# A gated-MLP times attention kernel: the order of the tiles and of their block sums ahead of the large product, and the lead of the last stage's loads

## The chip, the cores and the metric

The kernel runs on one core of one Trainium2 chip. The metric is the device time of one launch in microseconds, the median of the runs shown. A core has five engines with a queue of instructions each: TensorE (PE in the profile, with its weight loads as PEld), VectorE (DVE), ScalarE (ACT), GpSimd (POOL) and SyncE (SP), which here only issues the transfers. An engine takes its instructions in the order of its queue; an instruction at the head of a queue that has to wait holds up all those behind it.

## The reference

With x of 2048 rows by 512 columns, all in fp32:

```python
xn = _layernorm(x, axis=-1)
s = _A_ref(xn, A_k_cache, A_v_cache, A_wq, A_wo)      # attention: 32 heads, the last 512 keys
g = _silu(_B_ref(xn, B_w_in, B_w_sp, B_b_sp, B_w_out))
return x + s * g

def _B_ref(x, w_in, w_sp, b_sp, w_out):               # Fh = 688
    z = _gelu(jnp.einsum("bsd,df->bsf", x, w_in))
    z1 = z[..., :Fh]
    z2 = _layernorm(z[..., Fh:], axis=-1)
    g = jnp.einsum("ts,bsf->btf", w_sp, z2) + b_sp[None, :, None]
    return jnp.einsum("bsf,fd->bsd", z1 * g, w_out)
```

The change touches only B, from the computation of z2 on: z2 is 2048 x 688, w_sp is 2048 x 2048, w_out is 688 x 512.

## The kernel before, in words

A product of two fp32 operands is done with three matmuls: each operand is written as a high part (a cast to the matmul's type) and a low part (the operand less its high part), and high x high, high x low and low x high are summed. The cast is always done on ScalarE; the low part is always a subtraction in the helper of line 59, on VectorE or on GpSimd. So L59 stands for low parts of all kinds, and is told apart by shape and engine.

The order of the work is written out by hand: the order in which the code calls the operations is the order in each engine's queue. A table `ev` holds work by a time t (`on(t, f, ...)`); `step(t)` runs what stands under t. t counts the slots of the sweep (below), and the tiles of the z stage have the negative t, from -16 to -1.

**The z stage**, to 1509.9 us. 16 tiles of 128 rows, in the order of the list `ZO`: the lower half (tiles 8 to 15) first, then the upper half (0 to 7). A tile has two halves of 344 columns, each with 12 matmuls into a PSUM bank. ScalarE takes a half out of its bank with the gelu (L787), VectorE takes its statistics (L788, joined in L794). After every second tile, GpSimd computes 1/sqrt(var + eps) for the pair (L74, L75). The pairs of the lower half are then normalised on VectorE, in place (L802). For the pairs of the upper half GpSimd computes a shift (L804), and ScalarE normalises with it one tile later (`z_apply`, L809). Another tile later `z_split` makes high and low parts of the pair's left columns (L815 on ScalarE, L59 on GpSimd, tile `b`, 128x688).

**The sweep**, L873, 1509.9 to 1730.7 us. w_sp and z2 are cut into 2 x 2 blocks, called A11 to A22 and B11 to B22, and the product of the two is made of seven products of blocks (P1 to P7) in place of eight. For these, sums and differences of blocks are needed: T1, T2, T3, T4 on the side of z2 (`t_diff`, L887, on VectorE; `t_split`, L892 on ScalarE and L59), and sums of A blocks on the other (`a_sum`). Each block of z2 is held in four pieces j = 0 to 3 of two tiles of rows. The lower half of z2's rows gives B21 and B22, the upper half B11 and B12, so a difference of the two halves needs a piece of each. `t_diff` and `t_split` of the pieces stand in the event table.

The sweep has 56 slots (`SLOTS`), each of one product P and one tile of rows: 24 matmuls, eight pieces of three, into one of six banks `ps`. The first four slots multiply by B21 (P2), the next four by B11 (P1). A slot's operand of w_sp is prepared two slots ahead (`prep`: L858, cast on ScalarE, and L59 with 128x1024 elements on VectorE; for slots 0 and 1 the low part is done on GpSimd, in the z stage). `evict` takes the result of a slot out, at the following slot (L991 on ScalarE for P1, else VectorE). Finished rows of the gated product, u, are stored to `u_dram` (L979).

**The projection**, 1730.9 to the end. 16 tiles of rows in the order `PO`: tile n needs its rows of u, of s and of x. `load_p` fetches them with six transfers that SP issues (four of L1052 for u, one each of L1053 and L1054 for s and x) into a buffer of the pool `x8`, which has eight. `split_u` transposes u on VectorE (L1062, L1063) and makes high and low parts; `project` is 17 matmuls into a bank `ps_f`; `finish_out` is a Silu on ScalarE (L1082), a product on VectorE (L1083) and a sum on GpSimd (L1084), which leave the result in the tile's x8 buffer; `send_out` stores it from there (L1087). The first loads are issued in the last slots of the sweep, the others one for each tile.

The loop over the tiles at the end reads:

```python
for n, i in enumerate(PO):
    if n + 6 < NT: load_p(PO[n + 6])
    if n + 2 < NT: split_u(PO[n + 2])
    ...
    project(i); finish_out(i, nc.gpsimd)
    if n: send_out(PO[n - 1])
```

Of the kernel before, what the change touches and what calls it, by code (L numbers as in the profile page):

```python
# [12 lines left out]
OP = mybir.AluOpType  # L13
# [7 lines left out]
NT = S // P  # L21
# [13 lines left out]
T8 = NT // 2  # L35
# [5 lines left out]
def mixer_kernel(ctx: ExitStack, tc: tile.TileContext, x, wh, w_in, w_sp, b_sp, w_out, out):  # L41
# [8 lines left out]
    nc = tc.nc  # L50
# [101 lines left out]
    mv, rx, tmp = {}, {}, {}  # L152
# [391 lines left out]
    T0, T1 = -QL, NSTEP + OL  # L544
# [68 lines left out]
    n, t = 0, 28  # L613
# [138 lines left out]
    att.close()  # L752


    ZO = list(range(T8, NT)) + list(range(T8))
    RP = NT // 2
    HW = RP * P
    ctx.enter_context(tc.tile_pool(name="gap", bufs=1, side="right")).tile([P, 88], F32, name="gap")
    br = ctx.enter_context(tc.tile_pool(name="br", bufs=20, side="right", reuse_waits="tile"))
# [30 lines left out]
    def z_norm(pos):  # L790
        g, j = divmod(pos, 2)
        if j == 0:
            zmv[g] = stats.tile([P, 2, 2], F32, name="mvz")
        nc.vector.bn_aggr(zmv[g][:, j, :], zst[ZO[pos]])  # L794
        if j == 1:
            r = stats.tile([P, 2], F32, name="rz_r")
            tmp = stats.tile([P, 2], F32, name="rz_t")
            rsqrt(zmv[g][:, :, 1], r, 2, tmp)
            for k in range(2):
                t, mean, rs = zt(ZO[pos - 1 + k]), zmv[g][:, k, 0:1], r[:, k:k + 1]  # L800
                if pos < RP:
                    nc.vector.tensor_scalar(t, t, mean, rs, op0=OP.subtract, op1=OP.mult)  # L802
                else:
                    nc.gpsimd.tensor_scalar(tmp[:, k:k + 1], mean, rs, -1.0, op0=OP.mult, op1=OP.mult)  # L804
                    zn.setdefault(pos, []).append((t, tmp[:, k:k + 1], rs))

    def z_apply(pos):
        for t, shift, rs in zn.pop(pos, ()):
            nc.scalar.activation(t, t, AF.Identity, bias=shift, scale=rs)  # L809
# [87 lines left out]
    def on(t, f, *args):  # L897
        ev.setdefault(t, []).append((f, args))
# [3 lines left out]
    def step(t):  # L902
        if 1 < t + 2 < NS:
            prep(t + 2, V)
        for f, args in ev.get(t, ()):
            f(*args)

    for j in range(4):
        on((-8, -4, 4, 6)[j], load_halves, "P2", j)
        on((0, 2, 8, 10)[j], load_halves, "P1", j)  # L910
        on(-4 + 2 * j, t_diff, j, "T1")
        on(-4 + 2 * j, t_diff, j, "T3")
        on(-3 + 2 * j, t_diff, j, "T2")
        on(-3 + 2 * j, t_diff, j, "T4")
        on((-2, -1, 2, 4)[j], t_split, j, "T2", G if j == 2 else V)
    for j in range(4):
        on((0, 3, 5, 6)[j], t_split, j, "T1", V)
        on((1, 4, 12, 12)[j], t_split, j, "T3", V)
        on((13, 14, 17, 18)[j], t_split, j, "B22", V)
        on((18, 19, 20, 20)[j], t_split, j, "T4", V)  # L920
    AT = {0: (6, 7, 9, 10, 10, 11), 1: (12, 13, 15, 16, 16, 21), 2: (18, 20, 21, 23, 23, 25)}
    for r in range(RP):
# [6 lines left out]

    for pos, i in enumerate(ZO):  # L930
        for n in (2, 3):
            z_product(i, n)
            z_gelu(i, n)
        z_norm(pos)
        z_apply(pos - 1)
        if pos > 2 and pos % 2:
            z_split(pos - 2)
        if pos == 3:
            for k in ((0, 1), (1, 1)):
                fetch_x(0, k)  # L940
        t = pos - NT
        if t in (-6, -4):
            prep(t // 2 + 3, nc.gpsimd)
        step(t)
    left.close()
    psum.close()
# [143 lines left out]
    for k in range(NF):  # L1090
        on(WHEN[4, "P6"] + 2 if k < 2 else f7, load_wo, k)
        on(f7 + 2 + k // 3, split_wo, k)
    for n, t in enumerate((f7, f7, f7 + 1, f7 + 2, f7 + 3, f7 + 4)):
        on(t, load_p, PO[n])
    on(f7 + 3, split_u, PO[0])
    on(f7 + 4, split_u, PO[1])

    for t in range(NS):
        if t == 0:
            z_apply(NT - 1)  # L1100
        if t == 1:
            z_split(NT - 1)
        if t:
            evict(*SLOTS[t - 1])
        step(t)
        products(t)
# [2 lines left out]
        for f, args in ev.get(t, ()):  # L1109
            f(*args)  # L1110
    for n, i in enumerate(PO):
        if n + 6 < NT:
            load_p(PO[n + 6])
        if n + 2 < NT:
            split_u(PO[n + 2])
        if n == NT - 1:
# [50 lines left out]
```

## Time and profile before

| what | value |
|---|---|
| runs | 1807.52, 1811.16, 1806.87 us; median 1807.52 |
| profiled execution | 1810.7 us |
| its span, first to last instruction | 1808.9 us |
| mean granted clock of TensorE | 0.996 |
| busy: PE, DVE, ACT, POOL | 1775.6, 1491.2, 1177.4, 1260.5 us |
| attention and z1 | 0 to about 1451 us |
| z stage | about 1451 to 1509.9 us |
| sweep (L873) | 1509.9 to 1730.7 us |
| projection, `ps_f` | from 1730.9 us |

Everything up to 1451 us is the same in both kernels, and of no concern here. "The joint" is used below for the first slots of the sweep, where work on the last tiles of z still goes on. A row of the timeline reads: start in us, duration in us, engine, line, operation, tile written <- tiles read, shape, how many in a row; in brackets the idle time ahead of it and what ended it. A row of the table by windows gives for a stretch of time each engine's busy time, the clock granted to TensorE as a share of full speed, the busy share of the DMA engines, and GB/s. Rows of SPq are the issues of transfers on SP.

### The profile page before, as it was taken

Reading aid. Unit: us, or ns where it says so; the run is one execution under the profiler, and the core shown is the slowest. Engines: PE = TensorE matmul, PEld = TensorE weight load, DVE = VectorE, ACT = ScalarE, POOL = GpSimd, SP = SyncE. Lnnn points to the kernel's source line nnn. Section 1 sums busy time; section 2 is a strip of 40 time slices with the busy share of each in tenths; the row PEclk is TensorE's granted clock in tenths of the full one; section 3 lists DMA queues with packets and bytes.
Section 4 is the critical chain, followed back from the end, with each engine's and each line's share of the span. In section 5 each row is a group of like instructions: output and inputs, shape, how many; then the busy total and the mean of one; then the engine's idle time right before and its main releaser. Section 6 shows DMA issues by size and latency. Waiting matters only on the chain.

```text
span 1808.9 us, 28552 instructions
## 1 busy us (share of the span) xinstructions
PE 1775.6 (98%) x8460; PEld 1518.5 (84%) x8460; DVE 1491.2 (82%) x2447; ACT 1177.4 (65%) x2626; POOL 1260.5 (70%) x1199
## 2 busy tenths in 40 slices
PE   8999999999999999899999999999999999999997
PEld 7888888888888887788888888888888998999985
DVE  5689988989998988788888888888888557787774
ACT  4777777767777776577777777777777435443242
POOL 2798898898888987678888888888888324000042
PEclk9999999999999999999999999999999999999999
DMA  5687897988988889787877777777778643645476
GB/s 187 193 237 234 244 273 223 262 251 232 268 250 237 265 236 286 239 264 222 225 226 224 225 216 231 225 221 225 226 224 255 222 140 109 211 152 194 139 217 185
DMA packets 181164, 402.12 MB, mean 222 GB/s; under 512 B 24080, under 2 KB 61200, under 8 KB 161808
## 3 DMA queue, kind: packets, MB, share of 16 engines
q1 hardware_dynamic: 176400, 394.66, 73.5%
q10 hardware_dynamic: 4608, 5.64, 0.9%
q8 instruction: 66, 1.08, 0.2%
q14 instruction: 90, 0.74, 0.1%
HBM read 233.74 MB, written 166.46 MB: 221 GB/s over the span
## 4 chain that ended last, share of the span: by engine, by line
PE 82%; DMA 7%; DVE 4%; ACT 2%; SPq 2%; issue 2%; POOL 1%; ACTq 0%; DVEq 0%; POOLq 0%
PE ps_a L450 14%; PE ps L67 12%; PE ps L65 12%; PE ps L66 11%; PE ps L873 9%; PE ps_a L517 6%; PE ps_a L515 6%; PE ps_a L516 6%; PE ps_a L65 2%; PE ps_a L66 2%; PE ps_a L67 2%; DMA x<-x_dram 1%; DMA p_dram<-pL 1%; DMA pL<-p_dram 1%; DMA out<-x 1%
## 5 line engine op out<-in xcount | busy, mean ns | idle before, releaser
L59 POOL TENSOR_TENSOR pT_l<-pL,pT_h 128x512 fp32r<-128x512 f32 x507 | 658.4, 1302 | 187.5 <-ACT pT_h L507 165.7
L479 ACT ACTIVATE prob<-ps,nm 128x512 f32<-128x512 f32 x512 | 354.0, 691 | 339.7 <-DVE nm L477 332.2
L539 DVE SCALAR_TENSOR_TENSOR sacc<-ps,sums,sacc 128x512 f32<-128x512 f32 x496 | 369.8, 746 | 130.0 <-PE ps L67 124.4
L450 PE MATMUL ps_a<-x,x 128*128 128x512 f32 x1302 | 376.7, 390 | 6.1 <-DMA x<-x_dram 6.1
L488 DVE STREAM_TRANSPOSE pL<-prob 128x512 f32<-128x512 f32 x512 | 358.8, 701 | 3.3 <-ACT prob L479 3.3
L477 DVE TENSOR_REDUCE nm<-ps 128x1 f32<-128x512 f32 x512 | 340.1, 664 | 6.6 <-PE ps L67 6.5
L507 ACT CAST pT_h<-pL 128x512 fp32r<-128x512 f32 x512 | 318.5, 622 | 20.0 <-DMA pL<-p_dram 12.1
L450 PEld LDWEIGHTS ps_a<-x,x 128*128 128x128 f32 x1302 | 244.6, 188 | 58.1 <-DMA x<-x_dram 5.4
L59 POOL TENSOR_TENSOR wl<-raw,wh 128x512 fp32r<-128x512 f32 x186 | 242.0, 1301 | 11.9 <-ACT wh L144 11.9
L873 PE MATMUL ps<-b,x 128*128 128x344 f32 x1344 | 214.9, 321 | 6.2 <-ACT b L991 3.1
L873 PEld LDWEIGHTS ps<-b,x 128*128 128x128 f32 x1344 | 213.3, 189 | 7.7 <-ACT b L991 3.4
L517 PE MATMUL ps_a<-pT_l,wh 128*128 128x512 f32 x512 | 200.2, 391 | 2.3 <-POOL pT_l L59 2.2
L65 PE MATMUL ps<-wh,qT_h 128*128 128x512 f32 x512 | 199.9, 390 | 0.6 <-DVE sacc L539 0.6
L67 PE MATMUL ps<-wh,qT_l 128*128 128x512 f32 x512 | 200.0, 391 | 0.3
L515 PE MATMUL ps_a<-pT_h,wh 128*128 128x512 f32 x512 | 199.9, 390 | 0.0
L65 PE MATMUL ps<-wh,oT_h 128*128 128x512 f32 x512 | 199.7, 390 | 0.0
L66 PE MATMUL ps<-wl,qT_h 128*128 128x512 f32 x512 | 199.5, 390 | 0.0
L67 PE MATMUL ps<-wh,oT_l 128*128 128x512 f32 x512 | 199.5, 390 | 0.0
L66 PE MATMUL ps<-wl,oT_h 128*128 128x512 f32 x512 | 199.4, 390 | 0.0
L516 PE MATMUL ps_a<-pT_h,wl 128*128 128x512 f32 x512 | 199.3, 389 | 0.0
L59 POOL TENSOR_TENSOR b<-b 128x688 fp32r<-128x688 f32 (+1 forms) x11 | 19.2, 1747 | 198.1 <-ACT b L1039 189.7
L59 POOL TENSOR_TENSOR x<-wq,x 128x256 fp32r<-128x256 f32 x186 | 138.8, 747 | 1.5 <-ACT x L432 1.5
(207 smaller groups left out, 3010.8 us busy)
## 6 DMA issues: line engine op xcount, KB each, us to landing
p_dram<-pL SPq DMA_DIRECT2D x128, 1024.0 KB, 4.8
pL<-p_dram SPq DMA_DIRECT2D x256, 192.0 KB, 4.1
raw<-wh SPq DMA_DIRECT2D x188, 256.0 KB, 6.2
pL<-p_dram SPq DMA_DIRECT2D x256, 128.0 KB, 4.0
x<-w_sp SPq DMA_DIRECT2D x24, 1024.0 KB, 5.1
pL<-p_dram SPq DMA_DIRECT2D x256, 64.0 KB, 3.9
wq<-wh SPq DMA_DIRECT2D x62, 256.0 KB, 5.7
x_dram<-rawx SPq DMA_DIRECT2D x32, 256.0 KB, 6.1
```

The lines of the kernel that those rows point to most:

```text
L59: engine.tensor_tensor(lo, whole, hi.bitcast(F32), op=OP.subtract)
L65: nc.tensor.matmul(ps, lh, rh, start=first, stop=False)
L66: nc.tensor.matmul(ps, lh, rl, start=False, stop=False)
L67: nc.tensor.matmul(ps, ll, rh, start=False, stop=last)
L450: nc.tensor.matmul(qps[g, bank], wt["q", g, k][a][:, c * P:(c + 1) * P], X[g * 2 // H][ORDER[k]][:, b, c], start=first, stop=r == 5, skip_ ...
L477: nc.vector.tensor_reduce(nm, ps, axis=AX.X, op=OP.max, negate=True)
L479: nc.scalar.activation(prob[t], ps, AF.Exp, bias=nm, accum_out=sums[b][:, j:j + 1])
L488: nc.vector.transpose(pL[b][:, :, j * P:j * P + P].rearrange("p a (c q) -> p a c q", q=Q), prob.pop(t).rearrange("p (a c q) -> p a c q", a ...
L507: nc.scalar.copy(h, p)
L517: nc.tensor.matmul(pps[b], vh, pl, start=False, stop=c == 3)
L539: nc.vector.scalar_tensor_tensor(at, ps, rs, at, op0=OP.mult, op1=OP.add)
L873: nc.tensor.matmul(ps, a, b, start=k != "P4" and c == 0 and m == 0, stop=c == RP - 1 and m == 2, skip_group_check=True)
```

## The change

In the z stage:

- `ZO` takes pairs of tiles from the two halves in turn: 8, 9, 0, 1, 10, 11, 2, 3 and so on, to 14, 15, 6, 7. After each four tiles, a piece of each half is there.
- Every pair is normalised on ScalarE, with the shift from GpSimd; the normalisation on VectorE (L802 before) is gone.
- The differences of blocks stand at other times: for T1 and T3 at -10, -6, -2 and 3 in place of -4, -2, 0 and 2, for T2 and T4 at -9, -5, -1 and 4 in place of -3, -1, 1 and 3. The splits of T1, T2, T3 and B22 move too, and the one T2 split whose low part was on GpSimd has it on VectorE.
- The low parts of the operands of slots 0 and 1 are made on VectorE in place of GpSimd.
- Two blocks of the normalised x, which the tiles of the upper half multiply, are fetched back from DRAM (`fetch_x`) at position 5 in place of 3.

At the joint, the normalisation and the split of the last pair move from ahead of `evict` and `step` in slots 0 and 1 to events of slots 1 and 2. `step(t)` calls `prep(t + 2)` first, so these stand behind the operands of slots 2 and 3 on ScalarE and, for the split, of slot 4.

In the projection, loads are issued five tiles ahead, not six.

```diff
--- before.py
+++ after.py
@@ -752,8 +752,8 @@
     att.close()
 
 
-    ZO = list(range(T8, NT)) + list(range(T8))
     RP = NT // 2
+    ZO = [i + k for j in range(0, RP, 2) for i in (RP + j, j) for k in range(2)]
     HW = RP * P
     ctx.enter_context(tc.tile_pool(name="gap", bufs=1, side="right")).tile([P, 88], F32, name="gap")
     br = ctx.enter_context(tc.tile_pool(name="br", bufs=20, side="right", reuse_waits="tile"))
@@ -798,11 +798,8 @@
             rsqrt(zmv[g][:, :, 1], r, 2, tmp)
             for k in range(2):
                 t, mean, rs = zt(ZO[pos - 1 + k]), zmv[g][:, k, 0:1], r[:, k:k + 1]
-                if pos < RP:
-                    nc.vector.tensor_scalar(t, t, mean, rs, op0=OP.subtract, op1=OP.mult)
-                else:
-                    nc.gpsimd.tensor_scalar(tmp[:, k:k + 1], mean, rs, -1.0, op0=OP.mult, op1=OP.mult)
-                    zn.setdefault(pos, []).append((t, tmp[:, k:k + 1], rs))
+                nc.gpsimd.tensor_scalar(tmp[:, k:k + 1], mean, rs, -1.0, op0=OP.mult, op1=OP.mult)
+                zn.setdefault(pos, []).append((t, tmp[:, k:k + 1], rs))
 
     def z_apply(pos):
         for t, shift, rs in zn.pop(pos, ()):
@@ -905,18 +902,20 @@
         for f, args in ev.get(t, ()):
             f(*args)
 
+    on(1, z_apply, NT - 1)
+    on(2, z_split, NT - 1)
     for j in range(4):
         on((-8, -4, 4, 6)[j], load_halves, "P2", j)
         on((0, 2, 8, 10)[j], load_halves, "P1", j)
-        on(-4 + 2 * j, t_diff, j, "T1")
-        on(-4 + 2 * j, t_diff, j, "T3")
-        on(-3 + 2 * j, t_diff, j, "T2")
-        on(-3 + 2 * j, t_diff, j, "T4")
-        on((-2, -1, 2, 4)[j], t_split, j, "T2", G if j == 2 else V)
+        on((-10, -6, -2, 3)[j], t_diff, j, "T1")
+        on((-10, -6, -2, 3)[j], t_diff, j, "T3")
+        on((-9, -5, -1, 4)[j], t_diff, j, "T2")
+        on((-9, -5, -1, 4)[j], t_diff, j, "T4")
+        on((-8, -4, 3, 4)[j], t_split, j, "T2", V)
     for j in range(4):
-        on((0, 3, 5, 6)[j], t_split, j, "T1", V)
-        on((1, 4, 12, 12)[j], t_split, j, "T3", V)
-        on((13, 14, 17, 18)[j], t_split, j, "B22", V)
+        on((0, 1, 2, 5)[j], t_split, j, "T1", V)
+        on((0, 1, 2, 12)[j], t_split, j, "T3", V)
+        on((12, 13, 17, 18)[j], t_split, j, "B22", V)
         on((18, 19, 20, 20)[j], t_split, j, "T4", V)
     AT = {0: (6, 7, 9, 10, 10, 11), 1: (12, 13, 15, 16, 16, 21), 2: (18, 20, 21, 23, 23, 25)}
     for r in range(RP):
@@ -935,12 +934,12 @@
         z_apply(pos - 1)
         if pos > 2 and pos % 2:
             z_split(pos - 2)
-        if pos == 3:
+        if pos == 5:
             for k in ((0, 1), (1, 1)):
                 fetch_x(0, k)
         t = pos - NT
         if t in (-6, -4):
-            prep(t // 2 + 3, nc.gpsimd)
+            prep(t // 2 + 3, nc.vector)
         step(t)
     left.close()
     psum.close()
@@ -1090,16 +1089,12 @@
     for k in range(NF):
         on(WHEN[4, "P6"] + 2 if k < 2 else f7, load_wo, k)
         on(f7 + 2 + k // 3, split_wo, k)
-    for n, t in enumerate((f7, f7, f7 + 1, f7 + 2, f7 + 3, f7 + 4)):
+    for n, t in enumerate((f7, f7, f7 + 1, f7 + 2, f7 + 3)):
         on(t, load_p, PO[n])
     on(f7 + 3, split_u, PO[0])
     on(f7 + 4, split_u, PO[1])
 
     for t in range(NS):
-        if t == 0:
-            z_apply(NT - 1)
-        if t == 1:
-            z_split(NT - 1)
         if t:
             evict(*SLOTS[t - 1])
         step(t)
@@ -1109,8 +1104,8 @@
         for f, args in ev.get(t, ()):
             f(*args)
     for n, i in enumerate(PO):
-        if n + 6 < NT:
-            load_p(PO[n + 6])
+        if n + 5 < NT:
+            load_p(PO[n + 5])
         if n + 2 < NT:
             split_u(PO[n + 2])
         if n == NT - 1:
```

Since lines were taken out, line numbers behind them are lower by 3 in the z stage and the sweep (L809 is L806, L858 is L855, L892 is L889), and by 1 in the projection (L1052 is L1051, L1087 is L1086).

**GpSimd around the end of the z stage.** The rows L74, L75 and L804 (L801) are the rsqrt and the shift of a pair; L59 with 128x2x344 is the low part of a piece of z2, L59 with 128x1024 that of an operand of w_sp. Before:

```order
L75 TENSOR_TENSOR rz_r<-rz_t,power 128x2
L804 TENSOR_SCALAR rz_t<-mvz,rz_r 128x1 x2
L59 TENSOR_TENSOR b<-b 128x2x344
L59 TENSOR_TENSOR x_18683<-x_18524,x_18683 128x1024
L74 TENSOR_SCALAR rz_t<-mvz 128x2
L75 TENSOR_TENSOR rz_r<-rz_t,power 128x2
L804 TENSOR_SCALAR rz_t<-mvz,rz_r 128x1 x2
L59 TENSOR_TENSOR b<-b 128x2x344
L74 TENSOR_SCALAR rz_t<-mvz 128x2
L75 TENSOR_TENSOR rz_r<-rz_t,power 128x2
L804 TENSOR_SCALAR rz_t<-mvz,rz_r 128x1 x2
L59 TENSOR_TENSOR b<-b 128x2x344 x3
```

Now:

```order
L59 TENSOR_TENSOR b<-b 128x2x344
L74 TENSOR_SCALAR rz_t<-mvz 128x2
L75 TENSOR_TENSOR rz_r<-rz_t,power 128x2
L801 TENSOR_SCALAR rz_t<-mvz,rz_r 128x1 x2
L59 TENSOR_TENSOR b<-b 128x2x344
L74 TENSOR_SCALAR rz_t<-mvz 128x2
L75 TENSOR_TENSOR rz_r<-rz_t,power 128x2
L801 TENSOR_SCALAR rz_t<-mvz,rz_r 128x1 x2
L59 TENSOR_TENSOR b<-b 128x2x344 x2
```

The operand's low part is gone from this queue. Of the three low parts at the end before, the first two are the third and the fourth piece of B11, and the last is a piece of T2; of the two now, the first is the fourth piece of B21, the block that slot 0 multiplies, and the second the fourth piece of B11. The fourth piece of B21 thus stands behind the rsqrt and shift of the last pair; before, it was done in the middle of the z stage.

**ScalarE at the joint.** L787 is the gelu of a half tile, L809 (L806) the normalisation of a pair, L815 (L812) the high part of a piece of B21 or B11, L892 (L889) that of a difference, L858 (L855) that of a slot's operand. Before, with the operand of slot 2 in the last row:

```order
L787 ACTIVATE b<-ps_18734 128x344
L787 ACTIVATE b<-ps_18751 128x344
L809 ACTIVATE b<-b,rz_t,rz_r 128x2x344 x2
L892 CAST b<-b 128x2x344
L787 ACTIVATE b<-ps_18775 128x344
L787 ACTIVATE b<-ps_18791 128x344
L815 CAST b<-b 128x2x344
L892 CAST b<-b 128x2x344
L809 ACTIVATE b<-b,rz_t,rz_r 128x2x344 x2
L858 CAST x_18836<-x_18689 128x1024
```

Now:

```order
L787 ACTIVATE b<-ps_18752 128x344
L787 ACTIVATE b<-ps_18769 128x344
L806 ACTIVATE b<-b,rz_t,rz_r 128x2x344 x2
L787 ACTIVATE b<-ps_18791 128x344
L787 ACTIVATE b<-ps_18807 128x344
L812 CAST b<-b 128x2x344
L855 CAST x_18847<-x_18706 128x1024
L889 CAST b<-b 128x2x344 x2
L855 CAST x_18883<-x_18706 128x1024
L806 ACTIVATE b<-b,rz_t,rz_r 128x2x344 x2
```

The casts for the operands of slots 2 and 3 now stand ahead of the last pair's normalisation (the last row); before, they stood behind it.

**SP in the projection.** The number behind `x_` tells the x8 buffers' tiles apart; `out<-x_20573` and `out<-x_20581` are the store of tile 0, before and now. Before:

```order
L1052 DMA x_20828<-u_dram 32x4x192 x2
L1052 DMA x_20828<-u_dram 32x4x160 x2
L1053 DMA x_20828<-s_dram 128x512
L1054 DMA x_20828<-x 128x512
L1087 DMA out<-x_20573 128x512
L1052 DMA x_20865<-u_dram 32x4x192 x2
L1052 DMA x_20865<-u_dram 32x4x160 x2
L1053 DMA x_20865<-s_dram 128x512
L1054 DMA x_20865<-x 128x512
L1087 DMA out<-x_20580 128x512
```

Now:

```order
L1086 DMA out<-x_20581 128x512
L1051 DMA x_20866<-u_dram 32x4x192 x2
L1051 DMA x_20866<-u_dram 32x4x160 x2
L1052 DMA x_20866<-s_dram 128x512
L1053 DMA x_20866<-x 128x512
L1086 DMA out<-x_20588 128x512
L1051 DMA x_20903<-u_dram 32x4x192 x2
L1051 DMA x_20903<-u_dram 32x4x160 x2
L1052 DMA x_20903<-s_dram 128x512
L1053 DMA x_20903<-x 128x512
L1086 DMA out<-x_20625 128x512
```

With eight buffers, the load of tile 8 (`x_20865` before, `x_20903` now) takes the buffer of tile 0. Before, the store of tile 0 is the row just ahead of it; now a load and the store of tile 1 stand between the two.

## The prediction

> **What bounds the kernel now.** The page's first part says TensorE, and the windows by stage say where it does not.
>
> ```profile
> span 1808.9 us, 28552 instructions
> ...
> PE 1775.6 (98%) x8460; PEld 1518.5 (84%) x8460; DVE 1491.2 (82%) x2447; ACT 1177.4 (65%) x2626; POOL 1260.5 (70%) x1199
> ```
>
> ```profile
> core 0: us, PE busy (x) PEld busy (x) DVE busy (x) ACT busy (x) POOL busy (x), PEclk, DMA share, GB/s
> 1453.60:1509.94 56.34, 56.34 (x369) 56.34 (x368) 30.73 (x58) 26.53 (x47) 23.75 (x28) 1.00 0.27 94
> 1509.94:1540.00 30.06, 23.81 (x147) 22.39 (x145) 25.28 (x28) 15.32 (x21) 8.12 (x7) 1.00 0.48 149
> 1540.00:1543.40 3.40, 3.40 (x12) 3.40 (x13) 3.35 (x5) 3.40 (x5) 0.00 (x0) 0.50 0.46 184
> 1545.00:1705.00 160.00, 160.00 (x1016) 160.00 (x1015) 126.23 (x148) 60.24 (x67) 0.00 (x0) 1.00 0.52 174
> 1730.90:1769.49 38.59, 38.59 (x171) 31.86 (x171) 27.19 (x51) 15.38 (x30) 11.68 (x9) 1.00 0.73 203
> 1769.49:1800.58 31.09, 23.79 (x86) 17.71 (x84) 14.21 (x26) 7.51 (x16) 5.14 (x4) 0.89 0.67 197
> 1800.58:1808.90 8.32, 4.34 (x34) 4.14 (x34) 2.24 (x5) 0.74 (x2) 2.54 (x2) 1.00 0.39 144
> ```
>
> ```profile
> L873 PE MATMUL ps<-b,x x1344: 313/320/650, 1509.9 to 1730.7; 128*128 128x344 f32 x192
> ```
>
> The z stage (first row) has no gap on TensorE. The sweep's undisturbed pace is 160.00/1016 = 0.1575 us a matmul, so its 1344 matmuls (56 slots of 24) need 211.7 us; they stand from 1509.94 to 1730.90, the projection's first matmul, which is 220.96. **The joint loses 9.3 us.** A projection tile has 17 matmuls: ten take 38.59, or 3.86 each; the next five take 31.09 where five times 3.86 is 19.3. **The projection loses 11.8 us.** Its last tile and the way out take 8.32. All else is TensorE at its pace, so the change can win at these two places only. In the joint TensorE waits four times:
>
> ```profile
> 1518.91 0.58 PE L873 MATMUL ps<-b,x 128*128 128x344 f32 x2 [1.45 <-ACT x L858]
> 1520.17 4.05 PE L873 MATMUL ps<-b,x 128*128 128x344 f32 x24 [0.68 <-DVE x L59]
> 1525.15 11.68 PE L873 MATMUL ps<-b,x 128*128 128x344 f32 x70 [0.93 <-DVE x L59]
> 1539.92 5.27 PE L873 MATMUL ps<-b,x 128*128 128x344 f32 x22 [3.10 <-ACT b L991]
> ```
>
> Three waits are for a slot's operand, the fourth for ScalarE to empty a bank; behind the fourth the clock is 0.50 for 3.40 us (12 matmuls where 21.6 fit: 1.5 us lost). In the projection the chain runs through SP:
>
> ```profile
> 1741.84 0.38 SPq L1087 DMA_DIRECT2D out<-x  x1
> 1747.24 1.74 SPq L1052 DMA_DIRECT2D x<-u_dram  x4
> ...
> 1750.03 0.39 SPq L1087 DMA_DIRECT2D out<-x  x1
> 1753.76 1.74 SPq L1052 DMA_DIRECT2D x<-u_dram  x4
> ...
> 1756.55 0.38 SPq L1087 DMA_DIRECT2D out<-x  x1
> ```
>
> ```profile
> 1772.02 0.84 DVE L1062 STREAM_TRANSPOSE b<-x 128x640 f32<-128x640 f32 x1 [4.33 <-DMA x<-u_dram]
> 1775.63 0.80 PE L65 MATMUL ps_f<-b 128*128 128x512 f32 x1 [2.12 <-DVE x L1083]
> ```
>
> A load takes the buffer of the store issued just ahead of it, so SP sleeps through that store: store at 1750.03, load at 1753.76 (3.7 us), next store at 1756.55 (2.8 us of issues). That is 6.5 us a tile against TensorE's 3.86. The lead is used up by tile 11: VectorE waits 4.33 us for its u, everything behind stands, and TensorE waits in turn.
>
> **The change, part by part.**
>
> *Five ahead.* In the new order a load takes the buffer of the store before last: store k, load k+7, store k+1, load k+8. With L from a store's issue to its landing, a pair of tiles needs L + 2.8, so SP's period is (L + 2.8)/2: 3.25 us for L = 3.7, and 4.1 for the longest store in the rows (1741.84 to 1747.24, 5.4). What is late next is nothing: load 8 is in place at the same 1747.24 (store 0 must land), load 9 follows store 1 and load 8 at some 1750.5 instead of 1753.76, and each later one gains more. Tile 8's u is needed about 3.6 us (1772.02 to 1775.63) ahead of its matmuls at 1730.9 + 8 x 3.86 = 1761.8, and lands near 1751: 7 us of lead. At 4.1 a tile this shrinks by 0.24 a tile, 2 us in eight. One load fewer stands ahead of the sweep's end: load 5 moves behind the last stores of u, to where load 6 stands now, and is needed nearly 20 us later. All 11.8 us go, the two stretches of half clock in them included (0.89 in that window). Bounds: nothing (the wait stays) and 11.8, since the 3.86 and the 8.32 are TensorE and the way out. I take 11.8.
>
> *Tiles in turn.* The sum of rows is split over the z stage: half of its block differences stand in the joint today, a quarter then, and the operands of slots 0 to 3 are ahead of the normalisation of the last pair on ScalarE. The normalisation of the first half moves from VectorE to ScalarE.
>
> ```profile
> 1492.10 1.80 ACT L809 ACTIVATE b<-b,rz_t,rz_r 128x688 f32<-128x688 f32 x2
> 1493.80 1.03 ACT L858 CAST x<-x 128x1024 fp32r<-128x1024 f32 x1
> 1495.42 0.46 ACT L787 ACTIVATE b<-ps_a 128x344 f32<-128x344 f32 x1 [0.23 <-PE ps_a L67]
> 1495.78 0.76 ACT L815 CAST b<-b 128x688 fp32r<-128x688 f32 x1
> ```
>
> ScalarE's work for a pair of tiles is then 4 x 0.46 + 1.80 + 0.76, and where a difference is split and an operand prepared 0.76 + 1.03 more: 6.2 us, under the pair's 48 matmuls on TensorE, 56.34/369 x 48 = 7.3. It hides, with four banks between; if it did not, the fourth rival gives the price.
>
> What is new is a wait. P2, the first slot, multiplies block B21, the lower half. That half was done first; now its last quarter comes with the last tiles but two, and on POOL its low part stands *behind* the normalisation of the very last pair. POOL's steps, free and with VectorE beside them:
>
> ```profile
> 1489.40 0.22 POOL L74 TENSOR_SCALAR rz_t<-mvz 128x2 f32<-128x2 f32 x1 [4.72 <-DVE mvz L794]
> 1489.71 0.71 POOL L75 TENSOR_TENSOR rz_r<-rz_t,power 128x2 f32<-128x2 f32 x1
> ...
> 1490.98 1.67 POOL L59 TENSOR_TENSOR b<-b 128x688 fp32r<-128x688 f32 x1
> ...
> 1513.59 0.72 POOL L74 TENSOR_SCALAR rz_t<-mvz 128x2 f32<-128x2 f32 x1 [4.42 <-DVE mvz L794]
> 1514.39 1.31 POOL L75 TENSOR_TENSOR rz_r<-rz_t,power 128x2 f32<-128x2 f32 x1
> 1515.81 0.50 POOL L804 TENSOR_SCALAR rz_t<-mvz,rz_r 128x1 f32<-128x1 f32 x2
> 1516.27 1.66 POOL L59 TENSOR_TENSOR b<-b 128x688 fp32r<-128x688 f32 x1
> 1520.27 2.17 POOL L59 TENSOR_TENSOR b<-b 128x688 fp32r<-128x688 f32 x1 [2.34 <-ACT b L815]
> ```
>
> ```profile
> 1512.32 0.93 DVE L788 BATCH_NORM_STATS2 stz<-b 128x6 f32<-128x344 f32 x2
> 1513.28 0.21 DVE L794 BATCH_NORM_AGGREGATE mvz<-stz 128x2 f32<-128x12 f32 x1
> 1513.41 1.73 DVE L887 TENSOR_TENSOR b<-b 128x688 f32<-128x688 f32 x2
> ...
> 1518.89 1.23 DVE L59 TENSOR_TENSOR x<-x,x 128x1024 fp32r<-128x1024 f32 x1 [2.95 <-ACT x L858]
> ```
>
> TensorE does 18 of slot 0's 24 matmuls, to 1509.94 + 18 x 0.1575 = 1512.8, and then needs that low part. The order around the last pair's statistics is what it was (two differences, statistics, two differences), so I place them where they are: POOL's chain ends at 1516.27 + 1.66 = 1517.9. VectorE, idle there today, now has an operand and two splits to do, so the last step costs nearer 2.17, and the one before some 0.4 more: 1518.8, a wait of 6.0 us. Bounds: 5.1 (the row as it stands) and 9 (the first rival). A wait this long brings the half clock: 1.5 more.
>
> Do the other waits go? VectorE has, from 1513.4 to the operand of slot 5, two differences (1.73), four operands (4 x 1.23) and six splits (6 x 0.87): 11.9, with 3.3 for POOL's two steps of 1.67, to 1528.6; slot 5 starts at 1518.8 + 0.9 + 4 x 3.78 + 1.5 = 1536.3. By the fourth wait's place VectorE has one split, four differences and an operand more, 5.6 us, to 1534.2, ScalarE behind it frees the bank before slot 6 at 1540.1. They go. If the bank is late after all, 3.10 comes back. The two operands that go from POOL to VectorE (1.23 each) lie in the z stage, where VectorE is busy 30.73 of 56.34 us. The fetch of two blocks of x moves by two tiles, behind a z stage whose DMA share is 0.27: nothing.
>
> Joint: 9.3 goes, 6.0 + 1.5 comes, a gain of 1.8 (bounds -1.2 and 2.7).
>
> **Sum**: 1808.9 - 11.8 - 1.8 = 1795.3 for the span. The profiled execution took 1810.7, 1.8 over its span, and the median of the three runs is 1807.52; the saving of 13.6 taken from the median gives 1793.9, and I say **1794**.
>
> **Rivals.**
>
> 1. *POOL's steps are blocked, not slowed.* VectorE now has two-input work without a gap just then. If each of POOL's five instructions (0.22 + 0.71 + 0.50 + 1.67 = 3.1 us free) waits for a whole VectorE instruction of 0.87 to 1.23, the chain is 3.1 + 5 x 1.05 = 8.4 instead of 5.3 from 1513.5: a wait of 9, the joint gains nothing and loses 1.2, time 1797. For it: 0.22 became 0.72. Against: the whole chain, 1489.40 to 1492.65 free, took 1513.59 to 1517.93 beside VectorE: 1.1 more, not 5. The Trainium skill, page "SBUF — State Buffer", section "Who interferes with whom", calls the port pair that VectorE and GpSimd share an exclusive lock whose loser is blocked for the whole instruction; by that rule the sum would be this rival's, and the rows above, where no step waits for as much as it should in each case, agree in part.
> 2. *Stores land later, because loads and stores now overlap.* To bind, SP's period must pass 3.86 + 7/8 = 4.7, so L = 6.7 us; at L = 8, period 5.4, eight tiles lose 8 x 1.54 - 7 = 5.3 and a half clock 1.5: time 1801. Against: 5.4 is the longest L, with 0.73 of the DMA busy.
> 3. *The load takes another buffer than I count*, and SP sleeps as before: 1.8 gained, 1806, no change.
> 4. *The z stage becomes ScalarE's, and the kernel slower.* The normalisation sits in ScalarE's queue ahead of the next tile's gelu and waits for POOL. If POOL's chain is late each time as it once was in the rows below, statistics at 1503.83 and normalisation at 1507.33, ScalarE waits 3.3 a pair on top of its 6.2, over 7.3: 2.2 a pair. Then seven pairs lose 15 less the 5.5 that three banks of 1.84 (half a pair's half) cover once, and half clocks add 1.5 for each stop, six times: 9.5 + 9 = 18.5, time 1812. It decides where the wait passes 1.1 us a pair, 7.3 less 6.2. Against: two gelus, 3.7 us of TensorE, stand between statistics and normalisation, and today's second half does the same without a gap.
>
> ```profile
> 1503.83 0.21 DVE L794 BATCH_NORM_AGGREGATE mvz<-stz 128x2 f32<-128x12 f32 x1
> ...
> 1507.33 1.82 ACT L809 ACTIVATE b<-b,rz_t,rz_r 128x688 f32<-128x688 f32 x2 [0.40 <-POOL rz_t L804]
> ```
> 5. *The wait is short*: unblocked from 1509.94 (gelu 0.46, one statistic 0.93/2, 0.21, and 3.1) the low part is there at 1514.2, a wait of 1.4 and no half clock: 7.5 gained, 1788. Against: gelu and statistics of the last tile stand behind other work on both engines in the rows.
>
> **Numbers.** Forecast 0.70, rivals 0.13, 0.07, 0.03, 0.03, 0.04. The forecast's own spread is 1791 to 1797; with the first rival, and its wait a little longer, the range is 1790 to 1800; it leaves out rivals 2 to 5, 0.17. A difference below 0.3% (5.4 us) cannot be told from none. Faster 0.94 (forecast, 1, 2, 5), same 0.04 (3, part of 4), slower 0.02.
>
> **What would show it.** SP's loads and stores 3.3 to 4 us apart with no sleep of 3.7 behind each store; no wait of VectorE's transposes for u; projection tiles 3.86 apart to the last; one TensorE wait at 1512.8 for POOL's L59, about 6 us, then the clock at 0.50 for 3.4 us, and none up to the projection, which starts near 1729. Wrong would be: TensorE waiting for a bank in the z stage, waits for operands in slots 2 to 6, or a transpose waiting for u.

## The result, and the profile after

The changed kernel took 1799.12 us (median of six runs, 1798.36 to 1801.51) against 1809.92 of the kernel before (six runs, the three shown above among them). The ratio is 0.9944, with a 95% interval of 0.9931 to 0.9957: 10.8 us or 0.56% faster. The profiled execution took 1798.73 us with a span of 1796.9.

Where the 12.0 us between the two spans are, by stages (start of the sweep: first matmul of L873, now L870; start of the projection: first matmul into `ps_f`):

| stretch | before | after | gained |
|---|---|---|---|
| up to the start of the sweep | 1509.94 | 1508.81 | 1.1 |
| sweep | 220.96 | 222.03 | -1.1 |
| projection to the end | 78.0 | 66.1 | 11.9 |

The first row is no effect of the change: the first gelu of the z stage starts at 1453.8 in place of 1455.1, and the attention ahead of it is the same code. In twelve traces below that gelu starts anywhere from 1450.6 to 1455.8, so parts of the kernel are compared by their own lengths.

The projection, in the table by windows of the changed kernel, and the waits of SP from the sweep's end on, first before and then after:

```profile
1730.84:1769.40 38.56, 38.56 (x172) 31.87 (x171) 28.66 (x54) 16.41 (x32) 11.65 (x9) 1.00 0.91 269
1769.40:1788.25 18.85, 18.85 (x84) 15.59 (x84) 12.10 (x23) 6.62 (x13) 6.48 (x5) 1.00 0.62 200
```

```profile
SPq L1052 <- DMA out<-x: 26.3, 8, 4.5
```

```profile
SPq L1086 <- POOL x L1083: 13.3, 6, 3.4
...
SPq L1051 <- DMA out<-x: 0.8, 3, 0.3
```

TensorE has no gap in either window, and the clock is 1.00 in both. SP slept 26.3 us in eight loads that waited for a store to land (L1052 <- DMA out<-x); now 0.8. The 13.3 us that it waits for GpSimd's results at the stores (L1086 <- POOL) lie, but for 0.5, behind the issue of the last load (1773.81), so they hold no load up.

TensorE's timeline in the joint:

```profile
1508.81 3.07 PE L870 MATMUL ps<-b,x 128*128 128x344 f32 x19
1519.69 10.62 PE L870 MATMUL ps<-b,x 128*128 128x344 f32 x53 [7.80 <-POOL b L59]
```

The four waits of before are one, of 7.80 us, for a low part on GpSimd. GpSimd and VectorE at that place:

```profile
1512.59 0.72 POOL L74 TENSOR_SCALAR rz_t<-mvz 128x2 f32<-128x2 f32 x1 [3.00 <-DVE mvz L794]
1513.39 1.32 POOL L75 TENSOR_TENSOR rz_r<-rz_t,power 128x2 f32<-128x2 f32 x1
1514.81 3.23 POOL L801 TENSOR_SCALAR rz_t<-mvz,rz_r 128x1 f32<-128x1 f32 x2
1517.99 1.64 POOL L59 TENSOR_TENSOR b<-b 128x688 fp32r<-128x688 f32 x1
```

```profile
1512.41 1.73 DVE L884 TENSOR_TENSOR b<-b 128x688 f32<-128x688 f32 x2
1514.06 1.22 DVE L59 TENSOR_TENSOR x<-x,x 128x1024 fp32r<-128x1024 f32 x1
1515.19 1.65 DVE L59 TENSOR_TENSOR b<-b 128x688 fp32r<-128x688 f32 x2
1516.77 1.22 DVE L59 TENSOR_TENSOR x<-x,x 128x1024 fp32r<-128x1024 f32 x1
1519.71 1.66 DVE L59 TENSOR_TENSOR b<-b 128x688 fp32r<-128x688 f32 x2 [1.73 <-ACT b L889]
```

The two shifts (L801) took 3.23 us where they took 0.50 before. They end at 1518.0, when VectorE, which has run without a pause since 1512.4, stops for 1.73 us. The rows of the two shifts one by one, of VectorE's first low part, and of ScalarE's two normalisations, each of which waits for its shift:

```profile
1514.81 1.30 POOL L801 TENSOR_SCALAR rz_t<-mvz,rz_r 128x1 f32<-128x1 f32 x1
1516.08 1.95 POOL L801 TENSOR_SCALAR rz_t<-mvz,rz_r 128x1 f32<-128x1 f32 x1
1515.19 0.87 DVE L59 TENSOR_TENSOR b<-b 128x688 fp32r<-128x688 f32 x1
1516.14 0.96 ACT L806 ACTIVATE b<-b,rz_t,rz_r 128x688 f32<-128x688 f32 x1 [2.02 <-POOL rz_t L801]
1518.07 0.96 ACT L806 ACTIVATE b<-b,rz_t,rz_r 128x688 f32<-128x688 f32 x1 [0.96 <-POOL rz_t L801]
```

The first shift starts while VectorE makes an operand's low part (1514.06, 1.22 long) and ends at 1516.11, 0.05 us behind the end of VectorE's next instruction (1515.19 + 0.87 = 1516.06), while VectorE runs on. The second starts in the low part after that and ends at 1518.03, again 0.05 us behind the end of the next (1516.77 + 1.22 = 1517.99). So a shift, 0.27 us long by itself, lasted through the rest of the VectorE instruction in progress and the whole of the next one; it was not held until VectorE paused.

### The profile page after: what moved, and what is told of

Same layout as the page of the kernel before. It is cut to its first block, busy times and chain, and to the rows that moved or that the text cites. A ratio compares the mean times of both kernels' runs of the same rounds, so it can differ in the third digit from the quotient of the medians.

```text
span 1796.9 us, 28565 instructions
## 1 busy us (share of the span) xinstructions
PE 1770.7 (99%) x8460; PEld 1517.1 (84%) x8460; DVE 1482.9 (83%) x2442; ACT 1184.4 (66%) x2634; POOL 1258.9 (70%) x1204
## 3 DMA queue, kind: packets, MB, share of 16 engines
q8 instruction: 66, 1.08, 0.3%
## 4 chain that ended last, share of the span: by engine, by line
PE 89%; DVE 3%; DMA 3%; ACT 2%; issue 1%; POOL 1%; SPq 0%; ACTq 0%; DVEq 0%; POOLq 0%
PE ps_a L450 15%; PE ps L67 12%; PE ps L65 12%; PE ps L66 12%; PE ps L870 12%; PE ps_a L517 6%; PE ps_a L516 6%; PE ps_a L515 6%; PE ps_a L66 2%; PE ps_a L65 2%; PE ps_a L67 2%; DMA x<-x_dram 1%; PE ps_f L65 1%; PE ps_f L67 1%; PE ps_f L66 1%
## 5 line engine op out<-in xcount | busy, mean ns | idle before, releaser
L59 POOL TENSOR_TENSOR pT_l<-pL,pT_h 128x512 fp32r<-128x512 f32 x507 | 656.9, 1299 | 187.2 <-ACT pT_h L507 167.2
L59 POOL TENSOR_TENSOR wl<-raw,wh 128x512 fp32r<-128x512 f32 x186 | 241.5, 1298 | 11.9 <-ACT wh L144 11.9
L870 PE MATMUL ps<-b,x 128*128 128x344 f32 x1344 | 214.4, 321 | 7.8 <-POOL b L59 7.8
L870 PEld LDWEIGHTS ps<-b,x 128*128 128x128 f32 x1344 | 214.0, 189 | 8.1 <-POOL b L59 8.1
L59 POOL TENSOR_TENSOR b<-b 128x688 fp32r<-128x688 f32 (+1 forms) x10 | 17.2, 1727 | 198.3 <-ACT b L1038 195.8
L59 POOL TENSOR_TENSOR x<-wq,x 128x256 fp32r<-128x256 f32 x186 | 138.1, 743 | 1.5 <-ACT x L432 1.5
```

Source lines behind the costliest of these rows:

```text
L59: engine.tensor_tensor(lo, whole, hi.bitcast(F32), op=OP.subtract)
L870: nc.tensor.matmul(ps, a, b, start=k != "P4" and c == 0 and m == 0, stop=c == RP - 1 and m == 2, skip_group_check=True)
```

## The experiments

Twelve experiments, in three groups of four, each group on one chip with its own runs of the kernel before. Ratios are to these. The fourth, seventh and eighth were run once each, for the profile (1795.66, 1793.14 and 1796.59 us); of these only the rows are used.

**One part of the change alone.** The first experiment is the kernel before with

```diff
-    for n, t in enumerate((f7, f7, f7 + 1, f7 + 2, f7 + 3, f7 + 4)):
+    for n, t in enumerate((f7, f7, f7 + 1, f7 + 2, f7 + 3)):
-        if n + 6 < NT:
-            load_p(PO[n + 6])
+        if n + 5 < NT:
+            load_p(PO[n + 5])
```

> The kernel before with one edit: projection loads five tiles ahead instead of six. Theory A (the projection's 11.8 us were SP's sleep behind each store, and nothing else of the change is needed for them): VectorE's transposes wait for no load, projection tiles stay at 3.86 us to the last, 11.9 us gone, about 1798 against the kernel before's 1810 (ratio 0.9934); the joint keeps its four waits (6.2 us of idle TensorE, 9.3 us lost). Rival B (the tiles in turn are also needed, since they change what the sweep leaves to SP and the DMA queues): less than 8 us gone, ratio above 0.9955, and tiles over 5 us in the second half of the projection.

Measured: 1795.72 us against 1808.30, ratio 0.9930 (0.9903 to 0.9958). The windows from the sweep's first matmul to the projection, and from there to the end:

```profile
1510.52:1729.90 219.38, 214.18 (x1346) 213.32 (x1345) 175.00 (x203) 89.02 (x105) 17.24 (x13) 0.99 0.54 176
1729.90:1796.00 66.10, 62.10 (x291) 51.83 (x289) 43.17 (x81) 24.34 (x48) 19.45 (x15) 0.99 0.76 226
```

66.1 us, as in the changed kernel: theory A. This edit alone gives all that the change gives. The joint waited 5.2 us here, in three waits, where 6.2 in four were expected.

The second is the changed kernel with the same edit undone.

> The changed kernel with the projection loads put back to six ahead; the z stage and the joint stay as changed. Theory A (the new joint is worth nothing: its one wait of 7.8 us and the half clock behind it cost 10 us where the old four cost 9.3): 1811, ratio to the kernel before 1.0005 (0.9990 to 1.0015), the old waits of the projection back (span from the first matmul of the projection to the end 78, against 66). Rival B (the profile of the changed kernel was unlucky at the joint, and it does gain the forecast 1.8 us): 1808, ratio 0.9990 or lower, with a wait at slot 0 of 6 us.

Measured: 1809.24 us, ratio 1.0007 (0.9995 to 1.0019); the wait at slot 0 is 7.80 us again, the sweep 222.3 us, the projection 80.0 (78 were expected). Theory A: the tiles in turn and the new joint, taken by themselves, make no difference that can be measured.

The last experiment of the twelve belongs here: the changed kernel with loads four tiles ahead.

> The changed kernel with the projection loads four tiles ahead instead of five. Theory A (what mattered is that a load no longer takes the buffer of the store just ahead of it in SP's queue; two stores' distance is enough and the lead is not needed): the projection takes 66 us as with five, no wait of the transposes for u. Rival B (a shorter lead costs: the load of tile 8 is issued one tile later, and with loads landing 4 us and more after issue behind stores the lead of some 7 us is eaten): waits of the transposes for u return, the projection takes 68 us or more.

Measured: 1798.67 us, ratio 0.9943 (0.9925 to 0.9962).

```profile
1727.60:1793.70 66.10, 62.05 (x290) 51.81 (x289) 43.27 (x81) 24.32 (x48) 19.44 (x15) 1.00 0.76 230
```

66.1 us again, and no transpose waits for u. Theory A: what counts is the distance in SP's queue between a store and the load that takes its buffer, not the lead. A lead of six with one buffer more, which would change the distance alone, was not run.

**The wait at slot 0.** The third experiment moves the split of B21's fourth piece in the changed kernel:

```diff
     for pos, i in enumerate(ZO):
+        if pos == NT - 1:
+            z_split(pos - 2)
         for n in (2, 3):
...
         z_apply(pos - 1)
-        if pos > 2 and pos % 2:
+        if 2 < pos < NT - 1 and pos % 2:
             z_split(pos - 2)
```

> The changed kernel with one edit: the high and low part of the fourth piece of B21 are issued ahead of the last tile (ahead of its gelus on ScalarE, ahead of the last pair's rsqrt and shift on GpSimd). Theory A (the 7.8 us wait is that low part standing behind the last pair's chain on GpSimd, and nothing else is late near it): the low part is ready near 1512, the wait at slot 0 falls below 1 us, the half clock goes, 9 to 10 us gone against the changed kernel: 1789.5, ratio to the kernel before 0.9885. Rival B (the wait only covered others: the operands of slots 5 and 6 came at 1526.7 and 1530.4 in the changed kernel, and would be needed at 1527.7 and 1531.5 without the wait, a margin of 1 us): half of it comes back as waits at slots 2 to 8, about 1794, ratio 0.991.

Measured: 1794.18 us, ratio 0.9925 (0.9900 to 0.9950); the sweep takes 217.2 us. TensorE's timeline:

```profile
1508.92 3.07 PE L870 MATMUL ps<-b,x 128*128 128x344 f32 x19
1512.26 19.99 PE L870 MATMUL ps<-b,x 128*128 128x344 f32 x125 [0.27 <-POOL b L59]
1535.14 25.15 PE L870 MATMUL ps<-b,x 128*128 128x344 f32 x148 [2.88 <-ACT b L992]
```

The wait falls to 0.27 us as theory A says, but rival B is right on the rest: at slot 6 a wait of 2.88 us for a bank comes back, which the long wait had covered. 4.8 us are gained where 9 to 10 were expected.

The fourth takes two low parts out of VectorE's unbroken run:

```diff
-        on((0, 1, 2, 5)[j], t_split, j, "T1", V)
-        on((0, 1, 2, 12)[j], t_split, j, "T3", V)
+        on((1, 1, 2, 5)[j], t_split, j, "T1", V)
+        on((1, 1, 2, 12)[j], t_split, j, "T3", V)
```

> The changed kernel with the splits of the first piece of T1 and of T3 moved from slot 0 to slot 1, so that VectorE pauses near 1516.4 (after the operand of slot 3) instead of running without a gap to 1518.0. Theory A (GpSimd's two shift instructions, 3.23 us where they take 0.50 elsewhere, are held by VectorE's low parts running back to back, and get in when VectorE pauses): the two end near 1516.8, the wait at slot 0 is 1 to 1.3 us shorter (6.5 to 6.8). Rival B (they are held by something else): they take 3.2 us and the wait is 7.8 as it was.

Measured, on GpSimd and on VectorE:

```profile
1512.30 1.89 POOL L801 TENSOR_SCALAR rz_t<-mvz,rz_r 128x1 f32<-128x1 f32 x2
1514.15 1.64 POOL L59 TENSOR_TENSOR b<-b 128x688 fp32r<-128x688 f32 x1
```

```profile
1511.55 2.35 DVE L59 TENSOR_TENSOR x<-x,x 128x1024 fp32r<-128x1024 f32 x2
1516.49 3.23 DVE L59 TENSOR_TENSOR b<-b 128x688 fp32r<-128x688 f32 x4 [2.58 <-ACT b L889]
```

VectorE pauses at 1513.9 and the shifts end at 1514.2, 1.89 us long; the wait at slot 0 is 6.46, as theory A says to within 0.04. Taken one by one, the first shift lasts 1.66 us, from inside one operand's low part to 0.05 us behind the end of the next, and the second, beside an idle VectorE, 0.26. So VectorE's work holds the shifts, as theory A says; that it holds them until it pauses does not follow, since here the pause comes just behind the second of those two instructions.

The seventh puts differences among the low parts (`-1` becomes `0` in the third place of the times of `t_diff` for T2 and T4).

> The changed kernel with the differences of the third piece for T2 and T4 moved from ahead of VectorE's low parts to among them: behind the last statistics VectorE then runs the low part of slot 2's operand, two differences, two low parts, and the low part of slot 3's operand, again without a gap to 1518. Theory A (GpSimd's shift is held whatever VectorE runs, until VectorE pauses): the two shifts take 3 us and end when VectorE pauses, the wait at slot 0 stays at 7.8 us. Rival B (only VectorE's low parts hold GpSimd, its differences do not): the rsqrt's first step, now beside a low part, takes over 1 us, the shifts get in beside the differences and end near 1515.5, and the wait is 5.5 to 6.

Measured: the rsqrt's first step 1.11 us, the shifts 3.00, ending at 1518.4 where VectorE pauses; a wait of 7.84. These are theory A's numbers, and VectorE's differences do hold GpSimd as its low parts do: the rsqrt's second step, beside two differences, took 1.19 us where it takes 0.71 alone. But its "until VectorE pauses" is not what the rows show. The first shift starts inside a difference and ends at 1516.50, 0.05 us behind the low part that follows it, while VectorE runs on to 1518.4; the second lasts through the rest of one low part and the whole of the next, 1.95 us. In eight traces 15 shifts met such work of VectorE, and all 15 ended 0.05 us behind the VectorE instruction after the one in which they had started.

The eighth computes the last pair's two shifts on VectorE, where the two take 0.33 us.

> The changed kernel with the last pair's two shifts on VectorE (behind the low part of slot 2's operand) instead of on GpSimd, so that GpSimd goes from the rsqrt straight to the low part of B21's fourth piece, at 1514.8 by the rows of the changed kernel, while VectorE runs on to 1518. Theory A (every instruction of GpSimd is held until VectorE pauses): that low part ends at 1519.6 as before and the wait stays at 7.8 us. Rival B (the large subtraction gets its turns beside VectorE, as in the rows with 2.05 to 2.17 us; only the small shifts with a scalar operand from memory are held): it ends near 1517 and the wait is 5 to 5.5 us; VectorE's own low parts slow down in turn.

```profile
1513.95 1.31 POOL L75 TENSOR_TENSOR rz_r<-rz_t,power 128x2 f32<-128x2 f32 x1
1515.23 2.09 POOL L59 TENSOR_TENSOR b<-b 128x688 fp32r<-128x688 f32 x1
```

```profile
1515.99 2.85 DVE L59 TENSOR_TENSOR b<-b 128x688 fp32r<-128x688 f32 x2
```

Rival B, with a wait of 4.93 us where 5 to 5.5 were expected: the large subtraction gets in beside VectorE (2.09 us), and it is VectorE that pays, with 2.85 us for two low parts that take 1.65 otherwise; the first of them takes 2.06 and ends behind the subtraction. The subtraction waits for the rest of the VectorE instruction in progress and no longer, and VectorE's next then waits for it. The later one of this trace shows the same without any pause of VectorE: it starts at 1520.82 inside a low part, takes 2.26 us, and VectorE's next operand takes 2.69 instead of 1.22. So the shifts differ from GpSimd's other instructions here in that they let one more VectorE instruction pass; why, no run shows. The Trainium skill, page "SBUF — State Buffer", section "Who interferes with whom", says that the two engines share a pair of ports, and that a VectorE instruction with two inputs in SBUF contends with a GpSimd instruction that reads SBUF. The rows agree that they contend (3.23 against 0.50 us); that a shift waits for the end of two VectorE instructions, where a subtraction of 688 columns waits for the end of one, is what they add.

**A version that beats both.** The fifth is the third with three edits more: the last pair's shifts on VectorE (kept in the list `zsh`, computed by an event of slot 0), the last low part of B11 on VectorE, and the last differences for T2 and T4 one slot earlier.

```diff
+                if pos < NT - 1:
+                    nc.gpsimd.tensor_scalar(tmp[:, k:k + 1], mean, rs, -1.0, op0=OP.mult, op1=OP.mult)
+                else:
+                    zsh.append((tmp[:, k:k + 1], mean, rs))
...
-        rest(nc.gpsimd, lo, whole, hi)
+        rest(nc.vector if pos == NT - 1 else nc.gpsimd, lo, whole, hi)
...
-        on((-9, -5, -1, 4)[j], t_diff, j, "T2")
-        on((-9, -5, -1, 4)[j], t_diff, j, "T4")
+        on((-9, -5, -1, 3)[j], t_diff, j, "T2")
+        on((-9, -5, -1, 3)[j], t_diff, j, "T4")
```

> The changed kernel with four edits: the fourth piece of B21 split ahead of the last tile (as in the third experiment); the last pair's two shifts computed on VectorE behind the operand of slot 2 instead of on GpSimd; the last low part of B11 on VectorE instead of GpSimd; the last differences for T2 and T4 at slot 3 instead of 4. Theory A (the bank wait of 2.88 us that came back in the third experiment is ScalarE standing behind VectorE's block sums, which are late because GpSimd's shifts are held by VectorE, ScalarE's normalisation waits for them, and VectorE then waits for ScalarE): VectorE runs without the 1.7 us pause and without GpSimd beside it, the bank wait shrinks to 0.5 to 1.7 us, no half clock, the sweep from its first matmul to the projection takes 213 to 215 us against 222 in the changed kernel: 8 us gone against it, ratio to the kernel before about 0.9895. Rival B (the bank wait is VectorE's sum of work, not its pauses): the wait stays over 2.5 us, the sweep takes 217 as in the third experiment.

Measured: 1786.34 us against 1807.39, ratio 0.9893 (0.9872 to 0.9915); the sweep takes 213.2 us.

```profile
1507.88 3.08 PE L879 MATMUL ps<-b,x 128*128 128x344 f32 x19
1511.23 19.99 PE L879 MATMUL ps<-b,x 128*128 128x344 f32 x125 [0.27 <-POOL b L59]
1531.61 28.67 PE L879 MATMUL ps<-b,x 128*128 128x344 f32 x180 [0.39 <-ACT b L1002]
```

Two stops of 0.27 and 0.39 us are left. Theory A; what each of the three further edits is worth alone was not run. Beside it ran the changed kernel itself:

> The changed kernel itself, again, for a comparison on one chip with the version of the fifth experiment: ratio to the kernel before 0.994 as in its first runs (0.992 to 0.996), sweep 222 us, projection 66.

Measured: 1796.58 us, ratio 0.9948 (0.9928 to 0.9967); the sweep 222.6 us, the projection 66.1. The version of the fifth experiment is some 10 us faster on the same chip.

**The pace of the sweep.** In the seventh experiment the sweep took 215.7 us, 6.3 less than in the changed kernel, with the same wait at slot 0. The same window of both in the table by windows, where TensorE's busy time follows the window's length, with its matmuls in brackets; the changed kernel first:

```profile
1545.00:1705.00 160.00, 160.00 (x1016) 160.00 (x1016) 124.60 (x145) 59.66 (x66) 0.00 (x0) 1.00 0.53 176
```

```profile
1545.00:1705.00 160.00, 160.00 (x1046) 160.00 (x1045) 128.61 (x150) 63.19 (x69) 0.00 (x0) 1.00 0.53 176
```

1016 matmuls against 1046 in 160 us, at a clock of 1.00 in both: the starts lie 157.8 ns apart in the one and 153.3 in the other. The z stage, with matmuls of the same shape, has 153.3 ns in all traces, and so has the sweep up to TensorE's first stop: 48 matmuls in the kernel before and in the first experiment, 19 in the others. In nine of the first ten traces the pace is 157.8 ns from the first stop of TensorE to the end of the sweep. Two kernels were made for this.

> A kernel made for the pace of the sweep, with work left out: the low parts of nine pieces of T1, T2 and T3 are not computed (their high part is used in their place, so the output is not the reference's), which takes about 8 us off VectorE. Else as in the fifth experiment, with the low part of B21's fourth piece on VectorE, and the differences of the third pieces behind it, so that TensorE should find everything in place from the last tile of z to the projection. In nine traces so far the sweep's matmuls start 153.3 ns apart, as in the z stage, and go on 157.8 ns apart after TensorE's first stop, however short (0.27 us); in the seventh experiment they went on at 153.3 ns behind a stop of 7.84 us. Theory A (it is a stop that changes the pace): no stop, 153.3 ns to the end of the sweep, 1344 x 0.1533 = 206.1 us from its first matmul to the projection. Rival B (it is the work beside it, which starts with the sweep, or the place of the tiles): 157.8 ns from some 3 us into the sweep on, without a stop, 211 to 212 us.

> The kernel of the ninth experiment (same work left out) with one edit: the low part of B21's fourth piece is on GpSimd again, 1.67 us instead of 0.87, so that TensorE stops once, for 0.2 to 0.6 us, in slot 0. Theory A: 157.8 ns from that stop on, the sweep 5.5 to 6.5 us longer than in the ninth experiment, for a stop of less than 0.6. Rival B (the pace does not hang on stops): the same pace in both, and 0.2 to 0.6 us between them.

Between the two lies one condition, which sets the engine of one low part: `nc.vector if pos >= NT - 3` in the ninth, `nc.vector if pos == NT - 1` in the tenth. TensorE's timeline in the ninth and in the tenth, each with its window of 200 us:

```profile
1507.96 206.24 PE L881 MATMUL ps<-b,x 128*128 128x344 f32 x1344
```

```profile
1510.00:1710.00 200.00, 200.00 (x1306) 200.00 (x1305) 158.54 (x189) 87.16 (x102) 8.48 (x7) 1.00 0.58 184
```

```profile
1505.89 3.07 PE L881 MATMUL ps<-b,x 128*128 128x344 f32 x19
1509.25 209.32 PE L881 MATMUL ps<-b,x 128*128 128x344 f32 x1325 [0.29 <-POOL b L59]
```

```profile
1510.00:1710.00 200.00, 200.00 (x1269) 200.00 (x1269) 153.77 (x179) 84.11 (x97) 3.83 (x4) 1.00 0.55 178
```

Theory A. Without a stop, all 1344 matmuls keep 153.3 ns and the sweep takes 206.1 us (1507.96 to 1714.04); with one stop of 0.29 us it takes 212.5 (1505.89 to 1718.41). Of the 6.4 us between them, the slower pace behind the stop makes 1325 x 4.5 ns = 6.0, and the stop itself the rest. Each was run twice and profiled once: 1782.31 and 1782.62 us in the ninth, 1786.35 and 1790.40 in the tenth.

> The kernel of the seventh experiment again (differences among VectorE's low parts), to see whether its pace of 153.3 ns belongs to this kernel. If it belongs to the kernel: every run 5 to 6 us faster than the changed kernel, 1791 against 1797, ratio to the kernel before 0.991, and again 153.3 ns in the profile. If it was one execution's luck: as the changed kernel, ratio 0.9945, 157.8 ns.

Measured: 1798.52 us, ratio 0.9939 (0.9922 to 0.9955), and in its profile 1016 matmuls in the window above. It was one execution's luck: a stop can also leave the fast pace, as one of the thirteen traces with a stop shows.

## Why the prediction was right, and where it was wrong

- **Five ahead: right.** 11.8 us were to go from the projection, and 11.9 went; the mechanism (the distance between a store and the load into its buffer) is what the first and the last experiment show. SP's period, put at 3.25 to 4.1 us, is 4.1 (loads at 1740.68 and, eight later, 1773.81), but not for the reason given: half the landing of a store was to set it, and in these loads SP waited only 0.8 us for stores to land. That the number agrees is chance.
- **Tiles in turn hide in the z stage: right.** In the window of the z stage, first TensorE, then its weight loads, VectorE, ScalarE and GpSimd, TensorE has no gap; ScalarE is now busy 31.37 of 55.20 us. The fourth rival did not come, nor the second and the third (0.8 us of waits for stores).

```profile
1453.60:1508.80 55.20, 55.20 (x362) 55.20 (x361) 28.15 (x57) 31.37 (x55) 21.20 (x34) 1.00 0.25 85
```

- **The other waits go: right**, and for the reason given, that the wait at slot 0 comes first. The third experiment shows the price of that: take the wait away and the bank wait is back.
- **The wait at slot 0: wrong in the step that adds up GpSimd's chain**, "1518.8, a wait of 6.0 us". It was 7.80. Statistics and rsqrt came as reckoned, and the last low part cost 1.64, not 2.17. What failed is the 0.50 us of the two shifts: they took 3.23, each of them through the rest of one VectorE instruction and the whole of the next. That row of before stands in a stretch where VectorE had no work (1515.94 to 1518.89), and I moved it into a stretch where VectorE has no pause. The first rival had the mechanism, at a chance of 0.13, with a wait of 9; the forecast took GpSimd to be slowed only. The rival's 1.05 for each of five instructions is not right either: beyond their own time the two steps of the rsqrt waited 0.5 and 0.6, the shifts 1.0 and 1.7, the low part nothing, 3.8 in all. Its price for the joint, a loss of 1.2 us, is what came (1.1), but from other terms: a wait of 7.8 and a half clock of 2.0, not 9 and 1.5.
- **The half clock: too small.** 1.5 us was taken from a window of 3.40 us. Now the matmuls run at a clock of 0.50 from 1519.69 to 1523.80 (row below) and a little beyond, to 1524.1, and 2.0 us are lost: the 1325 matmuls behind the stop took 211.32 us, and 209.32 in the tenth experiment, without a half clock. How much is lost varies from execution to execution: by the same sum it is 1.5 to 2.6 in the five traces with a stop of 7.8 us and the pace of 157.8 ns. So the joint gives back 7.8 + 2.0 = 9.8, where 7.5 was forecast and 9.3 was to be gained: it loses.

```profile
1519.69:1523.80 4.11, 4.11 (x14) 4.11 (x15) 3.98 (x4) 4.11 (x6) 1.76 (x1) 0.50 0.27 59
```

- **The pace: a wrong reading with no effect on the sum.** "The sweep's undisturbed pace is 160.00/1016" is the pace after a stop. By the pace of the ninth experiment, 206.1 us for the sweep, the joint of before lost 15 us and not 9.3, of which some 6 hang on there being any stop. Both kernels have one, so it cancels; but what could be won in the joint was put too low, and a change that leaves no stop would be worth 6 us more than its waits.
- **The sum.** 13.6 us were forecast, and 10.8 measured: the joint lost 1.1 where 1.8 was to be gained. The rest of the way from 1794 to 1799.1 is the start: the median of the three runs was 1807.52, that of six 1809.92. The time lies near the upper end of the range of 1790 to 1800 and outside the forecast's own spread, 1791 to 1797; measured from the three runs that the forecast started from, a saving of 10.8 us is 1796.7. In the fifth rival the gain should read 9.3 - 1.4 = 7.9, not 7.5; its time stays at 1788.

## What to carry to other kernels

A duration is read together with what the neighbouring engine does in that row: a small instruction of GpSimd that takes 0.27 us beside an idle VectorE took 1.1 to 1.95 us beside a busy one here, so it does not belong in a chain that TensorE waits for. Where a load reuses a buffer that a store on the same queue frees, count how many instructions stand between the two; one store more in between was worth 11.9 us here. And before a pace is called undisturbed, compare it with that of the same matmul elsewhere in the kernel.

## What the runs showed of the hardware that was not expected

- TensorE has two steady paces for this matmul (344 columns, high and low parts alternating) at the same granted clock of 1.00, 153.3 and 157.8 ns. A stop of 0.27 us is enough to go from the first to the second, and it then holds for 200 us, to the end of the sweep. One stop of 7.84 us in one execution left the first. Which property of the stop decides was not settled.
- A small shift of GpSimd that started beside VectorE's block sums or low parts lasted through the instruction in progress and the whole of the next (1.08 to 1.95 us instead of 0.27, 15 of 15 in eight traces); the pair took 3.23 us in the changed kernel, 3.00 in the seventh experiment and 1.89 in the fourth. A large subtraction of GpSimd beside the same work let only the instruction in progress end; it took up to 2.26 us instead of 1.66, and VectorE's next instruction waited for it (two low parts 2.85 instead of 1.65).
